# Seven half-size products for eight in the first channel product of the last batch

## The chip, the cores and the metric

The kernel runs on one core of one Trainium2 chip. A core has five engines with instruction queues of their own, each working in the order in which its instructions were written: TensorE (PE, matrix products, which land in PSUM), Vector (DVE), Scalar (ACT), GpSimd (POOL) and SyncE (SP, which here only starts DMAs). PSUM has 16 KB for each of the 128 partitions, in eight banks of 512 fp32 columns. Products are read out of PSUM by Vector or Scalar; POOL works on SBUF alone in this kernel. The metric is the device time of one launch, in microseconds.

## The reference

Four batches, eight heads, 768 positions, head size 64. First comes attention in which each position sees a window of 128 positions and four sink positions; then a ResMLP block on the joined heads (`d_model` 512, hidden size 2048):

```python
x = attention(q, k, v)                      # (4, 768, 512)
a1 = alpha1 * x + beta1
u = x + lam * einsum('ts,bsd->btd', w_tok, a1)
a2 = alpha2 * u + beta2
out = u + lam * (maximum(a2 @ w_ch1, 0) @ w_ch2)
```

The change concerns `a2 @ w_ch1` of batch 3: 768 tokens by 512 channels times 512 by 2048.

## The kernel before

The kernel is a list of small tasks. Each task names the engines that may do it with a planner's cost for each, the tasks that it needs, and the buffers that it uses. Three tables fix everything in advance: `ORDER` (the order in which tasks are written into the engines' queues), `ENGINES` (which engine does each: a digit for ACT, DVE, PE, POOL, SP) and `HOMES` (which physical copy each buffer takes). `Plan.emit` (L54) walks `ORDER` and allocates each buffer from its pool when its first task is written. So no queue is sorted at run time, and an instruction that waits holds up all that were written behind it for its engine.

PSUM is one pool of six homes: four single banks `d` and two double banks `S`. Attention scores use `S`; all other products share `d`.

Batches overlap: while the channel products of batch b run, the attention of batch b+1 is mixed in. For batch 3 there is no next attention, so from its token products on only the ResMLP block remains. The stages of a batch that matter here:

- **Token product** (`tok`, L849): six tiles of six matmuls of 512 columns; Vector adds each to x (L868), Scalar or POOL casts the result to fp16 (L871), SP transposes it by DMA into `uT` (L920), and four affine steps for each half of 384 tokens apply alpha2 and beta2 (`uTx`, L914; the instructions are at L885 for Scalar and L887 for Vector).
- **First channel product** (`mlp1`, L933): for each half of 384 tokens and each of 16 slices of 128 hidden channels, four matmuls of 384 columns (L941) add up over the 512 channels in one `d` bank; one relu reads the bank and writes fp16 into `hT` (Scalar at L947 or Vector at L949). That is 32 groups of four matmuls and 32 relus.
- **Second channel product** (`prod`, L1022; matmuls at L1058): for batches 1 to 3 this is already done as seven half-size products P1 to P7 for eight (Strassen's scheme as Winograd orders it). Its sums over `hT` are made by Vector (`h_sums`, L983), its sums over `w_ch2` once, in batch 0 (`w2_sums`, L960; the instructions are at L973). Vector adds each product's bank to x (L1071, L1089 and others), and the rows are stored by DMA (L1077).

```python
for c in range(NC):
    nc.tensor.matmul(
        ph.t, w1f[:, c, fi * P : (fi + 1) * P],
        bu.t[:, c, chk * NTOK : (chk + 1) * NTOK], start=(c == 0), stop=(c == NC - 1))
```

In the written order, the last products of batch 2 (three each of P6, P5 and P3) stand between and behind the token tiles of batch 3, and the first groups of batch 3's channel product are mixed with the last of them.

Of the kernel before, what the change touches and what calls it, by code (L numbers as in the profile page):

```python
# [7 lines left out]
FP32 = mybir.dt.float32  # L8
# [25 lines left out]
class Plan:  # L34
# [19 lines left out]
    def emit(self, order, engines, homes, idles):  # L54
# [7 lines left out]
        for i in order:  # L62
# [6 lines left out]
            for b in t.uses:  # L69
                if b.t is None:  # L70
                    pool, shape, dtype = self.pools[b.kind]
                    b.t = pool.tile(b.shape or shape, b.dtype or dtype,
                                    tag=f"{b.kind}_{b.home}", bufs=1, name=b.name)
# [4 lines left out]
def kernel(  # L78
# [17 lines left out]
    nc = tc.nc  # L96
# [21 lines left out]
    ctx.enter_context(tc.manual_schedule())  # L118

# [19 lines left out]
        "S": (ps, [P, 2, 512], FP32),  # L139
# [3 lines left out]
        "rec": 2, "u16": 4, "uT": 1, "hT": 2, "wst": 4, "d": 4, "S": 2, "pt": 3, "tm": 1,  # L143
# [54 lines left out]
    for r in range(NR):  # L198
# [97 lines left out]
        "1111333333302002002132132002132002102020101212010321213120301212131201012121312010121213"  # L296
# [550 lines left out]
    pch = {}  # L847

    def tok(p, b, ti):  # L849
        pt = Buf("S" if (b, ti) == (0, 5) else "d", None, None, f"tok{b}_{ti}")  # L850
        bx = x[b, ti]

        def bank():
# [483 lines left out]
```

## Time and profile before

| | before |
|---|---|
| median of three runs | 253.14 us (252.94 to 253.52) |
| the profiled execution: its time | 252.88 us |
| its span, first to last instruction | 251.0 us |
| TensorE busy | 245.5 us, 2167 matmuls |
| Vector, Scalar, POOL busy | 192.7, 131.4, 107.0 us |
| matmuls of L941, all four batches | 512 |

The times are those of whole launches; the span is what the trace of one of them shows, and the 1.88 us between the two lie before the first and after the last instruction. In rows of instruction groups, "x77 | 36.7, 492 | 34.3" means 77 instructions, 36.7 us busy, 492 ns for one on average, and 34.3 us in which the engine stood idle just before one of them; an arrow names what ended most of that. In rows of the timeline the first two numbers are the start and the length in us, and a bracket at the end gives the idle time just before. Instructions of one kind that follow each other are merged there, with their count at the end; they overlap a little, so a row of three is shorter than three times the length of one. In rows of one source line, "414/424/1108" are the shortest, the median and the longest in ns.

### The profile page before, as it was taken

Reading aid. Unit: us, or ns where it says so; the run is one execution under the profiler, and the core shown is the slowest. Engines: PE = TensorE matmul, PEld = TensorE weight load, DVE = VectorE, ACT = ScalarE, POOL = GpSimd, SP = SyncE. Lnnn points to the kernel's source line nnn. Section 1 sums busy time; section 2 is a strip of 40 time slices with the busy share of each in tenths; the row PEclk is TensorE's granted clock in tenths of the full one; section 3 lists DMA queues with packets and bytes.
Section 4 is the critical chain, followed back from the end, with each engine's and each line's share of the span. In section 5 each row is a group of like instructions: output and inputs, shape, how many; then the busy total and the mean of one; then the engine's idle time right before and its main releaser. Section 6 shows DMA issues by size and latency. Waiting matters only on the chain.

```text
span 251.0 us, 5521 instructions
## 1 busy us (share of the span) xinstructions
PE 245.5 (98%) x2167; PEld 160.7 (64%) x2167; DVE 192.7 (77%) x402; ACT 131.4 (52%) x218; POOL 107.0 (43%) x125
## 2 busy tenths in 40 slices
PE   8899999999999999999999999999999999999994
PEld 8654655675555544566787686567667676657884
DVE  6798987778788886688789986677689985218884
ACT  2399935788986025687751445556660235543000
POOL 8818724967866516432872040065563130000010
PEclk9999999999999999999999999999999999999999
DMA  6999999999999996896479364420000136200025
GB/s 210 211 260 352 225 177 298 362 355 284 218 207 229 222 200 154 168 258 153 108 159 187 63 129 147 135 63 2 3 0 3 21 69 190 100 0 3 22 65 167
DMA packets 86561, 38.79 MB, mean 155 GB/s; under 512 B 73588, under 2 KB 81276, under 8 KB 86536
## 3 DMA queue, kind: packets, MB, share of 16 engines
q1 hardware_dynamic: 67696, 29.37, 49.4%
q10 hardware_dynamic: 15096, 5.80, 9.8%
q0 software_dynamic: 3744, 3.28, 8.2%
q8 instruction: 17, 0.28, 0.5%
q14 instruction: 8, 0.07, 0.1%
HBM read 29.91 MB, written 6.29 MB: 144 GB/s over the span
## 4 chain that ended last, share of the span: by engine, by line
PE 90%; ACT 4%; DVE 3%; issue 2%; DVEq 0%; ACTq 0%
PE h L941 32%; PE P L1058 22%; PE tok L861 12%; PE ch L1128 8%; PE pv L727 4%; PE S L626 4%; PE idle L148 2%; PE tp L516 1%; ACT wt L823 1%; ACT E L648 1%; DVE qkT L157 1%; PE S L621 1%; PE tp L513 1%; PE pv L720 1%; PE sk L558 1%
## 5 line engine op out<-in xcount | busy, mean ns | idle before, releaser
L941 PE MATMUL h<-uT,w1f 128*128 128x384 f16 x512 | 89.3, 326 | 0.1
L941 PEld LDWEIGHTS <-w1f 128*128 128x128 f16 x512 | 48.4, 98 | 31.9 <-issue 2.0
L947 ACT ACTIVATE hT<-h 128x384 f16<-128x384 f32 x77 | 36.7, 492 | 34.3 <-PE h L941 30.6
L949 DVE TENSOR_SCALAR hT<-h 128x384 f16<-128x384 f32 x51 | 27.4, 552 | 23.8 <-PE h L941 23.3
L1058 PEld LDWEIGHTS <-hT 128*128 128x128 f16 x408 | 39.3, 98 | 7.0 <-DVE hT L1001 0.7
L648 ACT ACTIVATE E<-S 128x1024 f16<-128x1024 f32 (+1 forms) x39 | 37.8, 1002 | 6.3 <-PE S L626 5.3
L771 POOL TENSOR_TENSOR tm<-x,la_b 128x512 f32<-128x512 f32 x18 | 24.7, 1372 | 22.2 <-DVE xh L774 12.0
L861 PE MATMUL tok<-xh,wtokT 128*128 128x512 f16 x144 | 33.2, 379 | 0.0
L1058 PE MATMUL P<-w2f,hT 128*128 128x256 f16 x216 | 26.7, 273 | 0.0
L155 ACT CAST u<-x 128x512 f16<-128x512 f32 x17 | 10.3, 616 | 28.0 <-DVE x L868 26.9
L1071 DVE TENSOR_TENSOR x<-x,P 128x256 f32<-128x256 f32 x45 | 18.1, 417 | 7.2 <-PE P L1058 6.6
L1094 POOL TENSOR_TENSOR x<-x,pt 128x256 f32<-128x256 f32 x4 | 4.0, 993 | 46.0 <-DVE pt L1089 46.0
L1058 PE MATMUL P<-w2s,hT 128*128 128x256 f16 x192 | 23.3, 273 | 0.0
L861 PEld LDWEIGHTS <-wtokT 128*128 128x128 f16 x144 | 13.8, 98 | 14.8 <-issue 0.2
L1128 PE MATMUL ch<-w2f,hT 128*128 128x512 f16 x96 | 22.7, 379 | 0.0
L753 DVE TENSOR_TENSOR x<-pv,rec 128x256 f32<-128x256 f32 x48 | 20.4, 425 | 1.7
L155 ACT CAST n<-nat 128x768 f16<-128x768 f32 x20 | 16.2, 830 | 8.5 <-DVE vs L580 6.6
L868 DVE TENSOR_TENSOR x<-x,tok 128x512 f32<-128x512 f32 x24 | 16.0, 682 | 3.7 <-PE tok L861 3.5
L727 PEld LDWEIGHTS <-E 128*128 128x128 f16 x328 | 15.2, 97 | 4.9 <-issue 1.1
L727 PE MATMUL pv<-vfs,E 128*128 128x65 f16 x328 | 17.7, 194 | 0.0
L588 POOL TENSOR_SCALAR_AFFINE_SELECT E<-E 128x512 f16<-128x512 f16 x12 | 8.8, 753 | 17.7 <-ACT E L648 17.7
L157 POOL CAST vfs<-vnat 128x512 f16<-128x512 f32 x18 | 13.4, 750 | 4.2 <-PE pv L727 4.2
(133 smaller groups left out, 338.9 us busy)
## 6 DMA issues: line engine op xcount, KB each, us to landing
wst_w<-in_moe_w_ch_dram SPq DMA_DIRECT2D x8, 512.0 KB, 7.2
nat<-in_q_dram SPq DMA_DIRECT2D x10, 384.0 KB, 4.2
nat<-in_k_dram SPq DMA_DIRECT2D x10, 384.0 KB, 8.0
vnat<-in_v_dram SPq DMA_DIRECT2D x14, 256.0 KB, 6.2
out_dram<-x SPq DMA_DIRECT2D x11, 256.0 KB, 3.1
wtn<-in_moe_w_tok_dram SPq DMA_DIRECT2D x6, 384.0 KB, 4.8
w1f<-in_moe_w_ch_dram POOLq DMA_DIRECT2D x4, 512.0 KB, 10.6
out_dram<-x ACTq DMA_DIRECT2D x7, 256.0 KB, 4.7
```

The source lines that it names most:

```text
L155: nc.scalar.copy(o, i)
L648: nc.scalar.activation(eT.t, pS.t[:, :, 0 : n * w].rearrange("p e (i w) -> p e i w", i=n), AF.Exp, scale=scale)
L727: nc.tensor.matmul(po.t[:, hl, :], eT.t[:, e_, off + i, c : c + P], vf[j][:, h, :], start=(r < 2 and n == 0), stop=(n == len(parts) - 1 an ...
L753: nc.vector.tensor_mul(bx.t[:, 4 * G : 4 * G + 4, :], po.t[:, :, 0:D], rec.t.to_broadcast([P, 4, D]))
L771: engine[e].tensor_mul(bt.t, bx.t.rearrange("p h d -> p (h d)"), la1_b)
L861: nc.tensor.matmul(bank(), wtokT[:, si, ti * P : (ti + 1) * P], hs[si].t, start=(si == 0), stop=(si == NR - 1))
L941: nc.tensor.matmul(ph.t, w1f[:, c, fi * P : (fi + 1) * P], bu.t[:, c, chk * NTOK : (chk + 1) * NTOK], start=(c == 0), stop=(c == NC - 1))
L947: nc.scalar.activation(bh.t[:, fi, :], ph.t, AF.Relu)
L949: nc.vector.tensor_scalar_max(bh.t[:, fi, :], ph.t, 0.0)
L1058: nc.tensor.matmul(pc.t, hh[:, nt * P : (nt + 1) * P], w(fi), start=(first and n_ == 0), stop=(n_ == HF - 1), skip_group_check=True)
L1071: nc.vector.tensor_add(row(bx)[:, cols], row(bx)[:, cols], pc.t)
L1128: nc.tensor.matmul(pc.t, bh.t[:, fi, nt * P : (nt + 1) * P], w2f[:, fi, :], start=(fi == 0), stop=(fi == NF - 1))
```

## The change

The weights and the input of batch 3's first channel product are each cut into four blocks: the 512 channels in two halves, the 2048 hidden channels in two halves, the 768 tokens in two halves. Eight block products are replaced by seven.

- **Sums of the weights** (`w1_sums`): S1 to S4, four sums or differences of blocks, each made in four pieces of 512 fp16 elements per partition: 16 instructions, all on Vector. They go into the four `wst` buffers, in which batch 3's q and k were staged. In the written order they stand in batch 2: three behind the last products of batch 1 (ahead of the relu that leaves Vector idle at 154 us in the trace before), two ahead of the next relus, seven about where Vector is idle at 161 us, and the last four behind the exponential of the fifth key block, ahead of the normalising at 179 us.
- **Sums of the input** (`u_sums`): T1 to T4, 768 fp16 elements per partition each, T1 and T2 on Vector, T3 and T4 on POOL, once all affine steps that they read are done.
- **Products** (`mlp1_pair`): slices i and i+8 of the hidden channels form a pair, eight pairs in all. A pair has seven groups of two matmuls of 384 columns. Four of them (P1, P6, P7, P4) go one after the other into one bank A, and the bank is read in between: copied into a second bank B (k1), copied to SBUF (k2), added to another product (a22), and passed through the relu (r21). P2 adds onto the copy in B (relu r11). P5 goes into a third bank, is copied to SBUF (k5), and P3 adds onto it (a12). The results of the two adds get their relu as a clip in SBUF. So a pair has seven reads of PSUM of 384 columns and two clips, where it had four relus. By the engine table the 56 reads are 31 on Scalar and 25 on Vector, and the 16 clips eight each on POOL and Vector, one Vector clip of them behind the last product of the pairs.
- **PSUM**: the double banks `S` get a pool of their own, opened first. When the first buffer of the new kind `A` is written, that pool is closed and a pool of four single banks opens in its place, with waits tile by tile. Two token tiles of batch 3, the fourth and the fifth, use `A` banks as well.
- **Order**: the six token tiles of batch 3 stand together, with nothing in between; nine products of batch 2 follow, with the first P1 groups of four pairs among the last of them. Two P1 products of the second channel product stand between the last groups of the pairs.
- **Other tasks**: three relus of batch 2 move from Vector to Scalar, two of them near 158 us and one at 177 us of the trace before; one piece of `w2_sums` (T1 of the last group, near 90 us) moves from Vector to POOL; three products of batch 2 take other `d` banks.

The tables `ORDER`, `ENGINES` and `HOMES` are left out of the diff here.

```diff
@@ -69,6 +69,9 @@
             for b in t.uses:
                 if b.t is None:
                     pool, shape, dtype = self.pools[b.kind]
+                    if callable(pool):
+                        pool = pool()
+                        self.pools[b.kind] = pool, shape, dtype
                     b.t = pool.tile(b.shape or shape, b.dtype or dtype,
                                     tag=f"{b.kind}_{b.home}", bufs=1, name=b.name)
             t.fn(e)
...
+    scope = tc.tile_pool(name="psS", bufs=1, space=bass.MemoryType.PSUM, reuse_waits="tile")
+    psS = scope.__enter__()
+
+    def single():
+
+        scope.__exit__(None, None, None)
+        return ctx.enter_context(
+            tc.tile_pool(name="psA", bufs=1, space=bass.MemoryType.PSUM, reuse_waits="tile"))
...
         "d": (ps, [P, 512], FP32),
-        "S": (ps, [P, 2, 512], FP32),
+        "S": (psS, [P, 2, 512], FP32),
+        "A": (single, [P, 512], FP32),
...
-        "rec": 2, "u16": 4, "uT": 1, "hT": 2, "wst": 4, "d": 4, "S": 2, "pt": 3, "tm": 1,
+        "rec": 2, "u16": 4, "uT": 1, "hT": 2, "wst": 4, "d": 4, "S": 2, "A": 4, "pt": 3, "tm": 1,
...
-        pt = Buf("S" if (b, ti) == (0, 5) else "d", None, None, f"tok{b}_{ti}")
+        pt = Buf({(0, 5): "S", (3, 3): "A", (3, 4): "A"}.get((b, ti), "d"), None, None, f"tok{b}_{ti}")
...
+    HPAIR = (3,)
+    aS = {}
+    uD = {}
+    def w1_sums(p):
+        a11, a12 = w1f[:, 0:2, 0 : DFF // 2], w1f[:, 2:4, 0 : DFF // 2]
+        a21, a22 = w1f[:, 0:2, DFF // 2 : DFF], w1f[:, 2:4, DFF // 2 : DFF]
+        for s in ("S1", "S2", "S3", "S4"):
+            aS[s] = Buf("wst", [P, 2, DFF // 2], FP16, f"w1{s}")
+        for s, sub_, i0, i1, need in (("S1", 0, a21, a22, None), ("S2", 1, "S1", a11, "S1"),
+                                      ("S3", 1, a11, a21, None), ("S4", 1, a12, "S2", "S2")):
+            for g in range(4):
+                f = slice(256 * g, 256 * g + 256)
+                def f_(e, s=s, sub_=sub_, i0=i0, i1=i1, f=f):
+                    r0, r1 = [aS[z].t if isinstance(z, str) else z for z in (i0, i1)]
+                    op = engine[e].tensor_sub if sub_ else engine[e].tensor_add
+                    op(aS[s].t[:, :, f], r0[:, :, f], r1[:, :, f])
+                done["a" + s, g] = add(
+                    p, {POOL: 2500, DVE: 700}, f_,
+                    [done["w1", i] for i in range(4)] + ([done["a" + need, g]] if need else []),
+                    [aS[s]] + ([aS[need]] if need else []), port=True)
+    def u_sums(p, b):
+        bu = uT[b, 0]
+        b11, b12 = (lambda: bu.t[:, 0:2, 0:NTOK]), (lambda: bu.t[:, 0:2, NTOK:S])
+        b21, b22 = (lambda: bu.t[:, 2:4, 0:NTOK]), (lambda: bu.t[:, 2:4, NTOK:S])
+        for s in ("T1", "T2", "T3", "T4"):
+            uD[b, s] = Buf("n16", [P, 2, NTOK], FP16, f"uD{b}{s}")
+        c11, c12, c21, c22 = [[(chk, c), (chk, c + 1)] for c in (0, 2) for chk in range(2)]
+        for s, i0, i1, need, parts in (("T1", b12, b11, None, c11 + c12), ("T2", b22, "T1", "T1", c22),
+                                       ("T3", b22, b12, None, c12 + c22), ("T4", b21, "T2", "T2", c21)):
+            def f_(e, s=s, i0=i0, i1=i1):
+                r0, r1 = [uD[b, z].t if isinstance(z, str) else z() for z in (i0, i1)]
+                engine[e].tensor_sub(uD[b, s].t, r0, r1)
+            done["u" + s, b] = add(
+                p, {DVE: 500, POOL: 1900}, f_,
+                [done["uT", b, chk, c] for chk, c in parts]
+                + ([done["u" + need, b]] if need else []),
+                [uD[b, s], bu] + ([uD[b, need]] if need else []), port=True)
+    def mlp1_pair(p, b, i):
+        bu = uT[b, 0]
+        if i == 0:
+            for chk in range(2):
+                hT[b, chk] = Buf("hT", None, None, f"hT{b}_{chk}")
+        h0, h1 = hT[b, 0], hT[b, 1]
+        k_ = i + NF // 2
+        bA = Buf("A", [P, NTOK], FP32, f"hA{b}_{i}")
+        bB = Buf("d", [P, NTOK], FP32, f"hB{b}_{i}")
+        bE = Buf("d", [P, NTOK], FP32, f"hE{b}_{i}")
+        bU = Buf("E", [P, NTOK], FP32, f"hU{b}_{i}")
+        bV = Buf("E", [P, NTOK], FP32, f"hV{b}_{i}")
+        A = lambda: bA.t
+        w = lambda c, f: w1f[:, c, f * P : (f + 1) * P]
+        g = i // 2
+        def mm(name, o, ws, xs, start, stop, after, uses):
+            def f_(e, name=f"{name}.{i}"):
+                for n_ in range(2):
+                    nc.tensor.matmul(o(), ws(n_), xs(n_), start=start and n_ == 0, stop=n_ == 1,
+                                     skip_group_check=True)
+            return add(p, {PE: 326}, f_, after, uses)
+        def tok_(c, chk):
+            return bu.t[:, c, chk * NTOK : (chk + 1) * NTOK]
+        def sums(s, n_):
+            return aS[s].t[:, n_, i * P : (i + 1) * P]
+        def relu(name, o, pt, after, uses):
+            def f_(e, name=f"{name}.{i}"):
+                if e == ACT:
+                    nc.scalar.activation(o(), pt(), AF.Relu)
+                else:
+                    nc.vector.tensor_scalar_max(o(), pt(), 0.0)
+            return add(p, {ACT: 395, DVE: 480}, f_, after, uses)
+        def plus(name, o, i0, i1, after, uses):
+            def f_(e, name=f"{name}.{i}"):
+                nc.vector.tensor_add(o(), i0(), i1())
+            return add(p, {DVE: 480}, f_, after, uses)
+        def clip(name, o, after, uses):
+            def f_(e, name=f"{name}.{i}"):
+                engine[e].tensor_scalar_max(o(), o(), 0.0)
+            return add(p, {POOL: 600, DVE: 250}, f_, after, uses, port=True)
+        w1_ = [done["w1", z] for z in range(4)]
+        B_ = lambda: bB.t
+        E_ = lambda: bE.t
+        c11, c21 = (lambda: h0.t[:, i, :]), (lambda: h0.t[:, k_, :])
+        c12, c22 = (lambda: h1.t[:, i, :]), (lambda: h1.t[:, k_, :])
+        half = [done["uT", b, 0, c] for c in range(NC)]
+        m1 = mm("P1", A, lambda n_: w(n_, i), lambda n_: tok_(n_, 0), True, True, w1_ + half, [bA, bu])
+        k1 = add(p, {ACT: 395, DVE: 480}, lambda e, k=f"k1.{i}": copy(e, bB.t, A()), [m1], [bA, bB])
+        m2 = mm("P2", B_, lambda n_: w(2 + n_, i), lambda n_: tok_(2 + n_, 0), False, True, w1_ + half + [k1], [bB, bu])
+        done["h", b, 0, i] = relu("r11", c11, B_, [m2], [bB, h0])
+        m6 = mm("P6", A, lambda n_: sums("S2", n_), lambda n_: uD[b, "T2"].t[:, n_], False, True,
+                [k1, done["aS2", g], done["uT2", b]], [bA, aS["S2"], uD[b, "T2"]])
+        k2 = add(p, {ACT: 395, DVE: 480}, lambda e, k=f"k2.{i}": copy(e, bU.t, A()), [m6], [bA, bU])
+        m5 = mm("P5", E_, lambda n_: sums("S1", n_), lambda n_: uD[b, "T1"].t[:, n_], True, True,
+                [done["aS1", g], done["uT1", b]], [bE, aS["S1"], uD[b, "T1"]])
+        m7 = mm("P7", A, lambda n_: sums("S3", n_), lambda n_: uD[b, "T3"].t[:, n_], False, True,
+                [k2, done["aS3", g], done["uT3", b]], [bA, aS["S3"], uD[b, "T3"]])
+        k5 = add(p, {ACT: 395, DVE: 480}, lambda e, k=f"k5.{i}": copy(e, bV.t, bE.t), [m5], [bE, bV])
+        a22 = plus("a22", c22, A, lambda: bV.t, [m7, k5], [bV, bA, h1])
+        done["h", b, 1, k_] = clip("r22", c22, [a22], [h1])
+        m4 = mm("P4", A, lambda n_: w(2 + n_, k_), lambda n_: uD[b, "T4"].t[:, n_], False, True,
+                w1_ + [a22, done["uT4", b]], [bA, uD[b, "T4"]])
+        done["h", b, 0, k_] = relu("r21", c21, A, [m4], [bA, h0])
+        m3 = mm("P3", E_, lambda n_: sums("S4", n_), lambda n_: tok_(2 + n_, 1), False, True,
+                [k5, done["aS4", g]] + [done["uT", b, 1, c] for c in range(NC)], [bE, aS["S4"], bu])
+        a12 = plus("a12", c12, E_, lambda: bU.t, [m3, k2], [bE, bU, h1])
+        done["h", b, 1, i] = clip("r12", c12, [a12], [h1])
...
+        if b in HPAIR:
+            m1 = [("us",)] + [("hp", i) for i in range(NF // 2)]
         seq += m1
+        if b == HPAIR[0]:
+            w1_sums(w0 - 50)
         if b in STRASSEN:
             def two(u, w):
                 return [("pr", a, nt) for a, nt in ((u, 0), (u, 1), (w, 0), (u, 2), (w, 1), (w, 2))]
 
             seq += two("P1", "P2")
-            i = seq.index(("m1", 1, 8))
+            i = seq.index(("pr", "P1", 0) if b in HPAIR else ("m1", 1, 8))
             seq[i:i] = [("hs", "S3")]
             i = seq.index(("pr", "P1", 0))
             seq[i:i] = [("hs", "S1")]
...
                 p -= PAR["hs"] if args[0] == "S3" else PAR["s2"]
             if what == "pr" and args[0] in ("P7", "P4"):
                 p -= PAR["p7"]
-            {"tok": tok, "uT": uTp, "m1": mlp1, "m2": mlp2, "hs": h_sums, "pr": prod}[what](p, b, *args)
+            {"tok": tok, "uT": uTp, "m1": mlp1, "m2": mlp2, "hs": h_sums, "pr": prod,
+             "us": u_sums, "hp": mlp1_pair}[what](p, b, *args)
```

More of the change, by code (lines that the diff above doesn't have):

```diff
@@ L295 @@
         "1212020212120202120212020212121202020202022221022221422221022221422221022221013111111331"
-        "1111333333302002002132132002132002102020101212010321213120301212131201012121312010121213"
+        "1311333333302002002132132002132002102020101212010321213120301212131201012121312010121213"
         "1203212131212131213421342104011121042104213400012120202021202021212120202020212120202121"
@@ L299 @@
         "4400004440443333330404040404040404020201012120101212133201012121312030121213120101212133"
-        "2032121312121312104210421040001210421042104000121212120212121212121202120202021202121202"
-        "0202020112120202020212020112021212121211111212121212121213121112131214214214210214214044"
+        "2032121312121312104210421040001210421042104000121212120212020212121202120202021202121202"
+        "0202020112020202020212020112021212121211111212121212121213121112131214214214210214214044"
         "4404404404433333304040404043404040202010121203012121312010121213320103212131203012121312"
-        "0321213321213121042104210410002104213421341010202021202120212120212020202020212020212120"
-        "2020201120202120212020201120202142021421411112121212121212111421110213142102142142142102"
-        "10"
+        "0321213321213111111111111111112104210421040011210421342134010111332021202201120211202120"
+        "2211320211202121220132121320202022013202112021212201120213202020220112021320202122013202"
+        "11202020220132021111112020210202142141111212121212121211302133021314210214210214210214"
     )
@@ L312 @@
         "103100135301020081002011411421050103321a003101204000011011051003031104020013001303110312"
-        "0021102210121102223200511310123320031102032021035337572302312010320101420152002210101311"
-        "162103012154110041003020b005101119102307200030023123011223130032122313100100121232070302"
-        "1202002102135312330203"
+        "0021102210121102223200511310123320031102132301035337572302312010320101420152002210101311"
+        "162103012154110041003020b005101119102307200010323002312203102012310101300213420235320230"
+        "01141123522003311247002301135231000210"
     )
```

54 rows, old and new, of the table ORDER are left out of this document.

## The prediction

> **What bounds the kernel now.** I read the page first, then the chain of waits from 190 us on, then the busy time by stretches.
>
> ```profile
> span 251.0 us, 5521 instructions
> PE 245.5 (98%) x2167; PEld 160.7 (64%) x2167; DVE 192.7 (77%) x402; ACT 131.4 (52%) x218; POOL 107.0 (43%) x125
> ...
> PEclk9999999999999999999999999999999999999999
> ...
> PE 90%; ACT 4%; DVE 3%; issue 2%; DVEq 0%; ACTq 0%
> ```
> ```profile
> 192.91 3.88 PE tok L861 x18
> ...
> 210.01 18.85 PE h L941 x116
> ...
> 231.26 16.61 PE P L1058 x152
> ```
> ```profile
> 190.00:198.00 8.00, 8.00 (x58) 5.29 (x56) 8.00 (x13) 0.75 (x2) 0.67 (x1) 1.00 0.01 2
> 198.00:207.70 9.70, 9.70 (x73) 6.87 (x71) 8.21 (x16) 3.32 (x6) 3.07 (x4) 1.00 0.35 68
> 207.70:231.10 23.40, 23.40 (x155) 14.86 (x153) 9.71 (x19) 11.59 (x25) 0.00 (x0) 1.00 0.22 74
> ```
>
> TensorE is the bound: 98% busy, 90% of the chain, full clock in every slice. In the last batch (columns of the third fence: PE, PEld, DVE, ACT, POOL busy, then clock and DMA) it has no gap between 190 and 231 us. Vector has room in the first channel product (9.7 of 23.4 us) and none ahead of it (8.0 of 8.0). From the chain come the paces: a 384-column matmul 18.85/116 = 0.1625 us, a 512-column one 3.88/18 = 0.216 us (a token tile of six 1.29 us), a 256-column one 16.61/152 = 0.109 us (a product of eight 0.87 us).
>
> **What the change removes.** The first product of batch 3 is 32 groups of four matmuls, 128 in all; it becomes 8 pairs of seven groups of two, 112. That is 16 x 0.1625 = **2.60 us** of TensorE, on the path. Everything else is added work on other engines; it costs what it makes TensorE wait.
>
> **Evacuations in the pair stretch.**
>
> ```profile
> L947 ACT ACTIVATE hT<-h 128x384 f16<-128x384 f32 x77 | 36.7, 492 | 34.3 <-PE h L941 30.6
> L949 DVE TENSOR_SCALAR hT<-h 128x384 f16<-128x384 f32 x51 | 27.4, 552 | 23.8 <-PE h L941 23.3
> ```
> ```profile
> 157.84 1.48 DVE L949 TENSOR_SCALAR hT<-h 128x384 f16<-128x384 f32 x3
> ...
> 221.10 1.79 ACT L947 ACTIVATE hT<-h 128x384 f16<-128x384 f32 x4 [0.81 <-PE h L941]
> ...
> 227.43 0.96 DVE L999 TENSOR_TENSOR hS<-hT,hT 128x1536 f16<-128x1536 f16 x1
> ```
> ```profile
> L1071 DVE TENSOR_TENSOR x<-x,P x45: 406/420/423, 127.5 to 247.9; 128x256 f32<-128x256 f32 x45
> L887 DVE TENSOR_SCALAR uT<-uT,ab x9: 368/371/375, 99.6 to 213.9; 128x384 f16<-128x384 f16 x9
> L157 POOL CAST u<-x x7: 609/611/938, 41.3 to 205.1; 128x512 f16<-128x512 f32 x7
> ```
>
> 32 evacuations of 384 columns become 56 (31 on Scalar, 25 on Vector by the engine table), plus 16 clips. Back to back, one costs Scalar (1.79 - 0.49)/3 = 0.43 us and Vector (1.48 - 0.55)/2 = 0.47 us. Copies that write PSUM, or fp32 to SBUF, and adds of an fp32 operand have no row at 384 columns; L1071 adds 256 columns in 0.42, below the relu's 0.55, so I give all the relu's pace and bound them by 0.55 without overlap. A clip (fp16, SBUF to SBUF) is nearest L887 on Vector, 0.37. On POOL it is bounded by 0.61 (a cast of 512) above and three quarters of it, 0.46, below; either is harmless, since POOL has eight in 18 us.
>
> TensorE's time here is 112 x 0.1625 = 18.2 us, and two P1 products of the second channel product are mixed in: 18.2 + 1.7 = 19.9 us. Scalar needs 31 x 0.43 = 13.3. Vector needs 25 x 0.47 = 11.8, seven clips 2.6, two channel sums (L999) 1.9, together 16.3. So 82%: it fits, with 3.6 us to spare, but Vector goes in order and is the tightest. A bank's own chain is four groups with a read after each: 4 x (0.33 for two matmuls + 0.2 until the read starts + 0.55) = 4.3 us, 0.2 as an estimate from product P at 231.97 + 0.87 and its add at 233.04 below; with four A banks a pair may finish every 1.1 us, where TensorE needs 2.3. So banks are no limit. I take 0.2 us for stalls here, of 0 to 2.6 (the upper end: every Vector evacuation 0.55, every Vector clip kept waiting a POOL clip of 0.61: 13.8 + 6.9 + 1.9 = 22.5 against 19.9).
>
> ```profile
> 231.97 1.04 PE L1058 MATMUL P<-w2f,hT 128*128 128x256 f16 x8
> ...
> 233.04 0.42 DVE L1071 TENSOR_TENSOR x<-x,P 128x256 f32<-128x256 f32 x1 [0.26 <-PE P L1058]
> ```
>
> That upper end rests on this pair, where a Vector sum ran 1.71 us instead of 0.96 beside a POOL multiply:
>
> ```profile
> 189.40 1.27 POOL L771 TENSOR_TENSOR tm<-x,la_b 128x512 f32<-128x512 f32 x1
> ...
> 189.78 1.71 DVE L1000 TENSOR_TENSOR hT<-hT 128x1536 f16<-128x1536 f16 x1
> ```
>
> The Trainium skill ("SBUF — State Buffer", Who interferes with whom) speaks against the clips too: it says that Vector's two-port modes, open to tensor_scalar, lock GpSimd out and the reverse, while an instruction with at most one SBUF input outside them is free. The nine L887 rows, 368 to 375 ns, show none held, so no row here decides it for clips; by the rule the seven could wait their 0.61 each, by the rows nothing, and the adds from PSUM (L1071, 423 ns at most) are free by both.
>
> **Getting there: token tiles and input sums.**
>
> ```profile
> 192.07 0.68 DVE L774 TENSOR_TENSOR xh<-tm,lb_b 128x512 f16<-128x512 f32 x1
> ```
> ```profile
> L868 DVE TENSOR_TENSOR x<-x,tok x24: 674/681/689, 33.5 to 204.9; 128x512 f32<-128x512 f32 x24
> L973 DVE TENSOR_TENSOR w2s<-w2f,w2s x7: 414/424/1108, 49.4 to 92.4; 128x512 f16<-128x512 f16 x7
> L973 POOL TENSOR_TENSOR w2f<-w2f x2: 1153/1154/1154, 97.4 to 101.9; 128x512 f16<-128x512 f16 x2
> ```
> ```profile
> L920 SPq DMA_TRANSPOSE uT<-u x6: 1192/1214/1267, 198.9 to 207.0; - x6
> L885 ACT ACTIVATE uT<-uT,ab x5: 692/696/706, 204.1 to 212.3; 128x384 f16<-128x384 f16 x5
> ...
> DMA to landing us min/median/max: 2.5/2.5/2.5
> ```
>
> All six token tiles now run in a row from 192.9 to 200.7, then nine products of batch 2 (7.9 us) to 208.6, then four P1 groups and a P2 to 210.2; only then does a group need a sum. On Vector the first u follows the addition at 192.07, three channel sums of batch 2 (0.96) and two adds (0.42): 192.75 + 3.7 + 0.68 = 197.1, cast by 197.7. The six transposes queue on SP at 1.21 each, so the sixth starts at 203.8 and lands at 206.3; two affines on Scalar end by 207.7, T1 and T2 on Vector (768 elements, 1.5 x 0.42 = 0.63 each) by 209.0. T3 and T4 on POOL (1.5 x 1.15 = 1.7 each) end by 209.4 and 211.1, before P7 and P4 of the first pair, each of which has a read and another group ahead of it. Cover 1.2 us, cost 0; were T2 later than that, the rest would show. The stores of batch 2 stand behind all six transposes on SP, as before.
>
> **The weight sums in batch 2.** Sixteen Vector sums of 512 fp16 elements, the shape of L973, 0.42 each: 6.7 us where TensorE is full.
>
> ```profile
> 154.16 1.02 DVE L949 TENSOR_SCALAR hT<-h 128x384 f16<-128x384 f32 x2 [1.22 <-PE h L941]
> 156.11 1.21 DVE L949 TENSOR_SCALAR hT<-h 128x384 f16<-128x384 f32 x2 [0.93 <-PE h L941]
> ...
> 161.64 0.56 DVE L949 TENSOR_SCALAR hT<-h 128x384 f16<-128x384 f32 x1 [1.73 <-PE h L941]
> ...
> 179.19 0.18 DVE L752 RECIPROCAL rec<-pv 128x4 f32<-128x4 f32 x1 [1.15 <-PE pv L727]
> ```
> ```profile
> 163.78 1.22 POOL L588 TENSOR_SCALAR_AFFINE_SELECT E<-E 128x512 f16<-128x512 f16 x2 [13.21 <-ACT E L648]
> ...
> 184.24 1.40 POOL L588 TENSOR_SCALAR_AFFINE_SELECT E_None<-E_None 128x1024 f16<-128x1024 f16 x1 [1.57 <-ACT E_None L648]
> ```
>
> The order puts three, two and seven of them at idle places of 1.22, 0.93 and 1.73 us, and two relus near the third go to Scalar (2 x 0.47): 12 x 0.42 = 5.0 against 4.8. POOL is idle there until 163.78, so nothing holds them. The last four (1.7) stand before the normalising at 179.19, with 1.15 idle and one relu moved: 1.6. Behind them wait the reciprocal, and behind it the bank of the next group. Excess 0.2 + 0.1; I take 0.4 of 0 to 1.0 for order.
>
> **The moved w2 sum** goes from Vector (0.42) to POOL (1.15), right behind this POOL multiply:
>
> ```profile
> 87.33 1.27 POOL L771 TENSOR_TENSOR tm<-x,la_b 128x512 f32<-128x512 f32 x1 [0.87 <-DVE xh L774]
> ```
> ```profile
> 88.80 0.68 DVE L774 TENSOR_TENSOR xh<-tm,lb_b 128x512 f16<-128x512 f32 x1
> 89.40 0.87 DVE L973 TENSOR_TENSOR w2s<-w2f,w2s 128x512 f16<-128x512 f16 x2
> ```
> ```profile
> 90.32 4.05 PE L861 MATMUL tok<-xh,wtokT 128*128 128x512 f16 x18
> ```
>
> If POOL goes first, the addition at 88.80, which the token product at 90.32 needs, ends 1.15 later than 89.48: 0.3 late; if it goes second, 0. I take 0.2.
>
> **The pool.** The A banks are first written by the fourth token tile, 192.7 + 3 x 1.29 = 196.6. The last score was read before POOL masked it at 184.24. Twelve us of cover, cost 0; without it, a drain.
>
> **The sum.** -2.60 + 0.2 (pairs) + 0.4 (weight sums) + 0.2 (moved sum) = **-1.8 us**. The profiled execution took 252.88, its span 251.0 and 1.88 around it: 249.2 + 1.88 = 251.1. The median shown is 0.26 above that execution, so **251.3**.
>
> **Rivals.**
> 1. Vector becomes the bound of the pairs: late adds hold A banks, P4 and P7 wait. For it: in-order queue, locks. Against: 16.3 of 19.9. At half of the 2.6 bound, in place of the 0.2: 252.4; at the bound 253.7.
> 2. The weight sums slow batch 2 by more than the product saves. L973's largest is 1108 ns, and the change's own table prices a weight sum at 700 where the same shape in w2 has 345. At one element a cycle (start to start 88.80 to 89.40, 0.60), 16 x 0.60 = 9.6 against 6.4 of gaps: 3.2 lost, -2.6 + 0.4 + 3.2 = +1.0, **254.1**. It decides from 16s - 6.4 = 2.2, a sum of 0.54 us. Against: type, shape and operation are those of 0.42.
> 3. The pool doesn't follow tile by tile but drains the engines at 196.6: Vector was full from 190 to 198, so about a sum and an add, 1.3 us: 252.6.
> 4. Short groups leave gaps and the granted clock falls. Half the clock for one slice of 6.3 us costs 3.1: 254.4. Against: 9 in every slice, where products with as many bank changes run. The Trainium skill ("TensorE: Matmul & The Clock Gate", A second HAM failure mode: psum-queue depth-cycling) describes such a case, with gaps between groups; no run here shows it.
>
> **Chances.** Forecast 0.66, own range 250.5 to 252.3; rivals 0.16, 0.12, 0.04, 0.02. Measurement tells about 0.2%, 0.5 us. Faster: 0.65 of the forecast, half of the first and third rival, 0.75; slower: 0.12 + 0.02 and the end of the first, 0.15; 0.10 between. Range 250.4 to 253.4: the rival at 254.1, the clock and edges fall outside.
>
> **What would show it.** L941-like matmuls 16 fewer at 0.1625; no TensorE gap between 205 and 229; weight sums at 0.42 and the batch-2 products at most 0.5 later; T2 done before the second group that needs a sum; POOL's w2 sum near 89. It is wrong if gaps stand ahead of groups that wait for Vector adds, if weight sums last over 0.54, or if the first batches move.

## The result, and the profile after

The changed kernel takes 250.74 us (median of five, 250.49 to 250.94) against 253.14 (252.94 to 253.52): a ratio of 0.990, 95% interval 0.989 to 0.992. It is faster, by 2.40 us in the medians; the span of the profiled execution fell by 2.6 us, from 251.0 to 248.4 (that execution: 250.51). The forecast was 251.3.

The first lines of the page of the changed kernel, with busy time of each engine, and its share of the chain of waits by engine:

```profile
span 248.4 us, 5583 instructions
PE 242.9 (98%) x2151; PEld 159.2 (64%) x2151; DVE 208.0 (84%) x437; ACT 136.1 (55%) x229; POOL 126.0 (51%) x139
...
PEclk9999999999999999999999999999999999999999
...
PE 90%; ACT 4%; DVE 3%; issue 2%; DVEq 0%; ACTq 0%
```

TensorE has 16 matmuls fewer (2167 to 2151) and 2.6 us less to do, and still holds 90% of the chain at full clock in every slice. Vector does 15.3 us more, POOL 19.0, Scalar 4.7; the chain's shares are the ones of before, and in the last batch, shown next, none of the added work is on it.

From the chain of waits of the changed kernel, in order of time (start, length, engine and line):

```profile
192.98 7.77 PE tok L880 x36
200.75 4.37 PE P L1199 x40
...
226.23 0.87 PE P L1199 x8
227.10 0.65 PE hA L1041 x4
227.75 17.48 PE P L1199 x160
245.23 0.02 issue
245.25 0.42 DVE x L1212
```

The token tiles of the last batch start at 192.98, 0.07 us later than before: all sixteen weight sums and the moved w2 sum lie ahead of this point, and left no mark beyond that. From there to TensorE's last matmul it is 245.23 - 192.98 = 52.25 us, before 247.87 - 192.91 = 54.96. So 2.71 us are gained in this stretch, 2.60 of them the 16 matmuls; the other 0.11 us lie in the nine products of batch 2, which by the pieces of the two chains took 8.04 us while they stood between the token tiles and take 7.93 now.

Busy time by stretches in the changed kernel (PE, PEld, DVE, ACT, POOL, then clock and DMA):

```profile
198.00:205.00 7.00, 7.00 (x54) 5.12 (x53) 6.78 (x12) 2.47 (x4) 2.12 (x4) 1.00 0.48 94
205.00:209.80 4.80, 4.80 (x42) 3.87 (x40) 4.80 (x12) 1.87 (x4) 2.54 (x2) 1.00 0.58 190
209.80:227.60 17.80, 17.80 (x115) 10.96 (x113) 16.58 (x36) 12.61 (x30) 12.01 (x10) 1.00 0.13 46
```

TensorE has no gap in any of them. In the pairs (the last row) Vector is busy for 16.58 of 17.80 us, 93%; POOL, idle there before, has 12.01.

### The profile page after: what moved, and what is told of

It is laid out like the page before. It is cut to its first block, busy times and chain, and to the rows that moved or that the text cites. A ratio compares the mean times of both kernels' runs of the same rounds, so it can differ in the third digit from the quotient of the medians.

```text
span 248.4 us, 5583 instructions
## 1 busy us (share of the span) xinstructions
PE 242.9 (98%) x2151; PEld 159.2 (64%) x2151; DVE 208.0 (84%) x437; ACT 136.1 (55%) x229; POOL 126.0 (51%) x139
## 4 chain that ended last, share of the span: by engine, by line
PE 90%; ACT 4%; DVE 3%; issue 2%; DVEq 0%; ACTq 0%
PE h L960 24%; PE P L1199 22%; PE tok L880 12%; PE ch L1269 8%; PE hA L1041 4%; PE pv L746 4%; PE S L645 4%; PE idle L161 2%; PE hE L1041 2%; PE tp L535 1%; ACT wt L842 1%; ACT E L667 1%; PE hB L1041 1%; DVE qkT L170 1%; PE tp L532 1%
## 5 line engine op out<-in xcount | busy, mean ns | idle before, releaser
L960 PE MATMUL h<-uT,w1f 128*128 128x384 f16 x384 | 68.0, 326 | 0.1
L960 PEld LDWEIGHTS <-w1f 128*128 128x128 f16 x384 | 35.9, 98 | 24.0 <-issue 2.0
L966 ACT ACTIVATE hT<-h 128x384 f16<-128x384 f32 x58 | 27.9, 492 | 21.5 <-PE h L960 17.9
L968 DVE TENSOR_SCALAR hT<-h 128x384 f16<-128x384 f32 x38 | 20.4, 553 | 8.1 <-PE h L960 7.7
L170 POOL CAST u<-x 128x512 f16<-128x512 f32 x7 | 4.6, 663 | 26.1 <-DVE x L887 16.9
L170 POOL CAST vfs<-vnat 128x512 f16<-128x512 f32 x18 | 13.9, 778 | 5.1 <-PE pv L746 4.2
```

What stands on the lines that cost most here:

```text
L170: engine[e].tensor_copy(o, i)
L960: nc.tensor.matmul(ph.t, w1f[:, c, fi * P : (fi + 1) * P], bu.t[:, c, chk * NTOK : (chk + 1) * NTOK], start=(c == 0), stop=(c == NC - 1))
L966: nc.scalar.activation(bh.t[:, fi, :], ph.t, AF.Relu)
L968: nc.vector.tensor_scalar_max(bh.t[:, fi, :], ph.t, 0.0)
```

## The experiments

The theory: the change is worth the 16 matmuls that it takes from TensorE, and all that it adds lies beside TensorE's work. The rivals: the additions do cost something that a gain elsewhere covers; or they were close to costing more (Vector in the pairs, the weight sums, the first input sums). For small effects I also compare a **stretch**, from the start of batch 2's first channel product to the start of Vector's last addition. It leaves out the loads of the first batches. Before it is 152.01 to 247.89, 95.88 us; in the changed kernel 152.10 to 245.25, 93.15. In the runs below the kernel before had a median of 253.47 us (first four) and 253.53 (last four). TensorE's waits are read in two ways. A bracket in a timeline gives its idle time; but a matmul's record reaches some 0.16 us past the start of the next one (eight of 384 columns last 1.46 us in the timeline, 1.30 by the pace), so a wait puts all later matmuls back by the idle time and up to 0.17 us more. I give this **shift** where it is needed: how much later than in the changed kernel a group starts, both counted from the start of the stretch.

**1. Sixteen matmuls put back.** The two matmuls of P1 in each pair are issued twice, the second time over the first; what is computed stays the same.

```diff
-                for n_ in range(2):
+                for n_ in (0, 1, 0, 1) if name.startswith("P1") else (0, 1):
```

> The changed kernel with each pair's P1 group issued twice into the same bank (the second time overwrites the first), so the 16 saved matmuls are back and everything else stays. Theory A (the time follows TensorE's issue time, all added work is covered): 16 x 0.1625 = +2.6 us on the changed kernel's 250.74, so 253.3, no different from the kernel before. Theory B (the pairs are already paced by their evacuations, TensorE only looks full): a part of the added matmuls fills waits, +1 us or less, 251.0 to 251.8.

Measured: 253.39 us, 1.000 of the kernel before (0.998 to 1.002). The stretch is 152.39 to 248.08, 95.69 us, 2.54 more than in the changed kernel. With TensorE's work put back the gain is gone, but for 0.19 us of the stretch: it is the matmuls, and all the rest of the change together is worth nothing that can be measured.

**2. All clips on Vector.** The engine table gives the eight clips of POOL to Vector.

```diff
-        "2211320211202121220132121320202022013202112021212201120213202020220112021320202122013202"
-        "11202020220132021111112020210202142141111212121212121211302133021314210214210214210214"
+        "2211120211202121220112121120202022011202112021212201120211202020220112021120202122011202"
+        "11202020220112021111112020210202142141111212121212121211302133021314210214210214210214"
```

> The changed kernel with the eight clips of POOL on Vector instead. A Vector clip took 0.25 us in the changed kernel, so Vector's 16.6 us between 209.8 and 227.6 become up to 18.6 of 17.8. Theory A (a sum over a stretch does not decide, only a matmul that waits does; the channel sums of 0.95 us each can slip behind the stretch): 250.7 to 251.2. Theory B (Vector is the bound of the pairs as soon as its sum passes the stretch): 250.74 + 0.8 or more, 251.5 to 252.5.

Measured: 250.96 us, 0.991 (0.987 to 0.994); the stretch is 93.17 us, 0.02 more. The pairs' stretch of this kernel, and its clips by line:

```profile
209.80:227.60 17.80, 17.80 (x115) 11.08 (x114) 17.33 (x43) 12.25 (x28) 3.31 (x2) 1.00 0.16 59
```
```profile
L1066 DVE TENSOR_SCALAR hT<-hT x16: 249/251/260, 213.8 to 230.0; 128x384 f16<-128x384 f16 x16
```

Eight clips more on Vector bring it to 17.33 of 17.80 us, 97%, and TensorE still has no gap: at this load Vector is not the bound yet. Having clips on POOL is not needed for the time.

**3. One copy of each pair from Scalar to Vector.** The copy k1 (the read of P1 that P2 waits for) goes from Scalar to Vector in all eight pairs.

```diff
-        "0321213321213111111111111111112104210421040011210421342134010111332021202201120211202120"
-        "2211320211202121220132121320202022013202112021212201120213202020220112021320202122013202"
-        "11202020220132021111112020210202142141111212121212121211302133021314210214210214210214"
+        "0321213321213111111111111111112104210421040011210421342134010111332121202201120211212120"
+        "2211320211212121220132121321202022013202112121212201120213212020220112021321202122013202"
+        "11212020220132021111112020210202142141111212121212121211302133021314210214210214210214"
```

> The changed kernel with the eight k1 copies (first bank to second bank) on Vector instead of Scalar: 8 x 0.47 = 3.8 us more on Vector, 20.4 in a stretch of 17.8. Theory A: some 2 us of channel sums and clips can slip behind the stretch, the rest shows as TensorE waiting for k1 before P2 and P6: +0.6 to 2.2, 251.3 to 252.9. Theory B: Vector's whole excess shows, 2.6 or more, 253.3 and up.

Measured: 252.53 us, 0.997 (0.996 to 0.999); the stretch is 152.43 to 247.13, 94.70 us, 1.55 more than in the changed kernel. Two stretches of time and, from the timeline, one group of matmuls with its wait:

```profile
205.00:209.80 4.80, 4.43 (x39) 3.53 (x37) 4.80 (x12) 1.31 (x2) 1.91 (x2) 1.00 0.42 131
209.80:229.50 19.70, 19.12 (x121) 11.60 (x120) 19.42 (x45) 9.86 (x23) 12.29 (x10) 1.00 0.15 56
```
```profile
214.91 0.48 PE L1041 MATMUL hA<-uD3T,w1S 128*128 128x384 f16 x2 [0.56 <-DVE hB L170]
```

Eight copies at 0.47 are 3.8 us more on Vector, and it is now busy 19.42 of 19.70 us. TensorE is idle for 0.37 us ahead of the pairs, where a product of batch 2 waits for a late Vector addition, and for 0.58 in them, 0.56 of it for a copy (hB). The shift grows by 0.47 us at the first of these waits, by 0.72 at the second and by 0.36 in small steps behind it: together the 1.55 of the stretch. Of 3.8 us, 1.55 showed, so some 2.2 still found cover: Vector's room in the changed kernel is between the 1.2 us that it is idle in the pairs and these 2.2.

**4. Each weight sum made twice.** The sum is written a second time over itself; the result stays the same.

```diff
-                    op(aS[s].t[:, :, f], r0[:, :, f], r1[:, :, f])
+                    for _ in range(2):
+                        op(aS[s].t[:, :, f], r0[:, :, f], r1[:, :, f])
```

> The changed kernel with each of the 16 weight sums in batch 2 made twice: 16 x 0.34 = 5.4 us more on Vector. By the count of idle places (6.4 us, of which 5.4 are taken already): 4.4 us lost, 255.1. If the banks and the work written ahead give TensorE more slack than the idle places show, less: +1 to 3, 251.7 to 253.7. If Vector's place in batch 2 does not matter at all: 250.7.

Measured: 260.32 us, 1.028 (1.025 to 1.032); the stretch is 102.69 us, 9.54 more than in the changed kernel and far more than expected. Two things were missed. First, the price of a repeated sum: from the timelines of Vector, the changed kernel, then this one:

```profile
160.23 1.43 DVE L993 TENSOR_TENSOR w1S<-w1f 128x512 f16<-128x512 f16 x4
```
```profile
153.58 2.47 DVE L994 TENSOR_TENSOR w1S<-w1f 128x512 f16<-128x512 f16 x6
163.47 4.01 DVE L994 TENSOR_TENSOR w1S<-w1f 128x512 f16<-128x512 f16 x8
183.86 4.00 DVE L994 TENSOR_TENSOR w1S<-w1f,w1S 128x512 f16<-128x512 f16 x8
```

In the changed kernel each sum after the first costs (1.43 - 0.42)/3 = 0.34 us. A repeat starts only after the sum whose place it writes again has ended, so a sum and its repeat take 0.34 + 0.45 us from start to start; that gives the 2.47 us for six. The rows of eight are longer for another reason: in each of them two sums last 0.85 and 0.74 us instead of 0.42, while POOL is at work on a mask, which in the changed kernel comes when the sums are done. The sums of this kernel by line, and that work of POOL:

```profile
L994 DVE TENSOR_TENSOR w1S<-w1f x16: 416/424/852, 153.6 to 166.7; 128x512 f16<-128x512 f16 x16
L994 DVE TENSOR_TENSOR w1S<-w1f,w1S x8: 411/424/853, 183.9 to 187.4; 128x512 f16<-128x512 f16 x8
```
```profile
165.66 1.55 POOL L607 TENSOR_SCALAR_AFFINE_SELECT E<-E 128x512 f16<-128x512 f16 x2 [14.37 <-ACT E L667]
185.24 1.55 POOL L607 TENSOR_SCALAR_AFFINE_SELECT E<-E 128x512 f16<-128x512 f16 x2 [1.85 <-ACT E L667]
```

In all Vector does 9.0 us more (208.0 to 217.0), not 5.4; its time in weight sums rises from 5.7 to 14.0. Second, the clock. TensorE in the changed kernel, and the same two groups here:

```profile
163.83 1.46 PE L960 MATMUL h<-uT,w1f 128*128 128x384 f16 x8
...
166.00 0.61 PE L645 MATMUL S<-qkT 64*128 64x256 f16 x8
```
```profile
168.33 2.79 PE L960 MATMUL h<-uT,w1f 128*128 128x384 f16 x8 [2.56 <-DVE x L1213]
...
172.08 0.61 PE L645 MATMUL S<-qkT 64*128 64x256 f16 x8
```

And the stretches around that wait and around a second one (the column after POOL is the granted clock):

```profile
164.70:168.11 3.41, 1.07 (x5) 0.39 (x4) 3.32 (x7) 0.88 (x1) 2.45 (x4) 1.00 0.00 0
168.11:171.52 3.41, 3.19 (x14) 1.43 (x14) 2.42 (x6) 0.62 (x1) 0.40 (x1) 0.50 0.00 0
171.53:174.94 3.41, 3.41 (x43) 2.42 (x42) 2.33 (x8) 1.69 (x4) 1.84 (x2) 1.00 0.43 117
185.18:188.59 3.41, 1.15 (x18) 0.76 (x15) 3.20 (x8) 1.82 (x3) 1.55 (x2) 1.00 0.00 0
188.60:192.01 3.41, 3.41 (x12) 1.60 (x11) 1.97 (x5) 0.00 (x0) 1.26 (x1) 0.50 0.00 0
```

TensorE stood for 2.56 us, and then the granted clock was 0.50 for 3.41 us: eight matmuls took 2.79 us instead of 1.46. Against the changed kernel the first group is 168.33 - 163.83 = 4.50 us late and the second 172.08 - 166.00 = 6.08, so the low clock cost 1.58 us beside the wait. A second wait of 2.26 us did the same (0.50 for 3.41 us, 1.68 us lost). The waits themselves come to 6.3 us (shifts of 0.60, 0.56, 2.72 and 2.42), the clock to 3.3: 9.6, the 9.5 measured. The mean granted clock of this execution, 0.987, says the same: 1.3% of 258.6 us is 3.4. It is not always as much: of the four executions two had 0.987 and 0.986 (260.66 and 261.07 us), and two 0.993 (259.79 and 259.99), half the loss of clock.

**5. Only one set of weight sums made twice.** Since run 4 mixed the two, the four sums S3 alone are repeated.

```diff
-                    op(aS[s].t[:, :, f], r0[:, :, f], r1[:, :, f])
+                    for _ in range(2 if s == "S3" else 1):
+                        op(aS[s].t[:, :, f], r0[:, :, f], r1[:, :, f])
```

> The changed kernel with only the four pieces of S3 made twice: 4 x 0.4 = 1.6 us more on Vector at the third idle place of batch 2 (160 to 162 us). Without a slack beyond the idle places (2.7 us there with the two moved relus, of which seven sums take 2.4): 1.3 us lost, 252.0. If free banks and what is written ahead carry TensorE on for half a microsecond or more, as in the doubled run, where 1.4 us more on Vector cost TensorE 0.5: 0.4 to 0.9 lost, 251.1 to 251.6.

Measured: 252.21 us, 0.996 (0.994 to 0.997); the stretch is 152.84 to 247.20, 94.36 us, 1.21 more, for 1.8 us more work on Vector. TensorE on the timeline of this kernel, and the stretch around:

```profile
165.07 0.81 PE L960 MATMUL h<-uT,w1f 128*128 128x384 f16 x4 [0.35 <-DVE x L1213]
...
166.40 0.82 PE L960 MATMUL h<-uT,w1f 128*128 128x384 f16 x4 [0.51 <-DVE x L772]
```
```profile
164.00:167.00 3.00, 2.14 (x12) 0.90 (x11) 2.90 (x7) 0.53 (x1) 2.39 (x4) 1.00 0.00 0
```

Groups of matmuls wait for ordinary additions that now come late behind the sums, and the clock stays at 1.00 through gaps of this size. The shift is 0.51 us at the first of these waits and 1.18 after the second. Against the idle places of the prediction (6.4 us) the account by the time of all weight sums on Vector is: 5.7 us, no loss; 7.4, a loss of 1.2; 14.0, 6.3 of waiting. So the loss starts about where the places are full. Closer than that the three kernels don't tell, since a sum fits or not at its own place: at the third (2.7 us, of which seven sums take 2.4) the 1.8 us more would lose 1.5, and 1.2 were lost.

**6. Two token tiles back in the shared banks.** Token tiles 3 and 4 of the last batch take d banks, as in the kernel before, instead of A banks.

```diff
-        pt = Buf({(0, 5): "S", (3, 3): "A", (3, 4): "A"}.get((b, ti), "d"), None, None, f"tok{b}_{ti}")
+        pt = Buf({(0, 5): "S"}.get((b, ti), "d"), None, None, f"tok{b}_{ti}")
```

> The changed kernel with the fourth and fifth token tile of batch 3 in d banks (2 and 3) instead of A banks of the pool that follows the scores'. In the changed kernel the second token tile, which holds bank 2, was read by Vector until about 197.2, and the fourth would start at 196.7. If those two A banks carry a part of the gain: TensorE waits 0.5 us there, 251.2 (251.0 to 251.5). If the banks of the token tiles do not matter: 250.7.

Measured: 251.66 us, 0.992 (0.990 to 0.995); the stretch is 93.83 us, 0.68 more. The token tiles on TensorE's timeline, of the changed kernel and then of this one:

```profile
192.82 7.93 PE L880 MATMUL tok<-xh,wtokT 128*128 128x512 f16 x36
```
```profile
197.70 4.05 PE L880 MATMUL tok<-xh,wtokT 128*128 128x512 f16 x18 [0.48 <-DVE x L887]
```

With A banks all six tiles follow each other; with d banks the fourth waits 0.48 us for Vector's addition that empties its bank, a shift of 0.65 and the only wait of TensorE in this stretch. So a part of the pool's worth is in the token tiles, not in the pairs. And nothing drained at the change of pools: the fourth tile, the first to write an A bank, has no gap ahead of it.

**7. The first two input sums on POOL.** T1 and T2 go from Vector to POOL.

```diff
-        "0321213321213111111111111111112104210421040011210421342134010111332021202201120211202120"
+        "0321213321213111111111111111112104210421040011210421342134010133332021202201120211202120"
```

> The changed kernel with the input sums T1 and T2 on POOL, in front of T3 and T4 there. POOL's T4 took 1.64 us, so T1 to T4 end at about 209.6, 211.2, 212.9 and 214.5 where they ended at 208.5, 209.3, 210.8 and 212.4. Theory A (only the cover of T2 counts, 0.8 us in the changed kernel): the first P6, which started at 210.14, waits until 211.3, and P7 a little more: +1.2 to 2.0, 251.9 to 252.7. If what is written ahead gives more slack than that: 250.7.

Measured: 252.73 us, 0.996 (0.994 to 0.998); the stretch is 94.70 us, 1.55 more. The first group that needs a sum, on TensorE's timeline, and POOL's rows of T1, T2 and T3:

```profile
212.04 0.48 PE L1041 MATMUL hA<-uD3T,w1S 128*128 128x384 f16 x2 [1.08 <-POOL uD3T L1013]
```
```profile
208.56 1.65 POOL L1013 TENSOR_TENSOR uD3T<-uT 128x768 f16<-128x768 f16 x1 [1.97 <-ACT uT L904]
210.29 1.70 POOL L1013 TENSOR_TENSOR uD3T<-uT,uD3T 128x768 f16<-128x768 f16 x1
211.95 1.64 POOL L1013 TENSOR_TENSOR uD3T<-uT 128x768 f16<-128x768 f16 x1
```

The group waits for T2, which ends at 211.99, and starts at 212.04, a shift of 1.25 us; T3, which ends at 213.59, adds 0.30 to it ahead of the group at 213.64. These two are the 1.55. In the changed kernel T2 ends on Vector at 209.34 and that group starts at 210.14, with no wait: 0.8 us of cover.

**8. The late block read first.** In batch 1's token tiles the matmul of the sixth block, the one that reads the addition that stands behind the moved w2 sum, goes first instead of last. The sums are the same, in another order.

```diff
-                for si in sis:
+                last = NR - 1
+                for si in [last] + list(range(last)) if b == 1 else sis:
```

> The changed kernel with the six matmuls of each token tile of batch 1 in another order: the one that reads the last addition to xh goes first instead of sixth. If the moved w2 sum was free because only the sixth matmul waits for that addition: the first token product of batch 1, at 90.34 in the changed kernel, now waits until the addition has ended at 90.46 and starts 0.15 to 0.3 later, and the time grows by that much at most. If the token product waited as a whole already, nothing moves.

A single execution: 250.63 us, span 248.6. Vector's addition and TensorE in the changed kernel (two engines), then here:

```profile
88.82 1.64 DVE L793 TENSOR_TENSOR xh<-tm,lb_b 128x512 f16<-128x512 f32 x1
...
90.34 4.05 PE L880 MATMUL tok<-xh,wtokT 128*128 128x512 f16 x18
```
```profile
88.91 1.64 DVE L793 TENSOR_TENSOR xh<-tm,lb_b 128x512 f16<-128x512 f32 x1
...
90.60 4.04 PE L881 MATMUL tok<-xh,wtokT 128*128 128x512 f16 x18
```

In the changed kernel the addition ends at 88.82 + 1.64 = 90.46 and the token product starts at 90.34, ahead of it: only the sixth matmul of a tile reads it, and that one's turn comes at 90.34 + 5 x 0.216 = 91.42, so nothing waits. With the order turned, the first matmul starts at 90.60, just after the addition's end at 90.55, and 0.17 us after the 20 matmuls ahead of it were issued (86.11 + 20 x 0.216 = 90.43). One time as a whole can't tell 0.17 us; the row does.

## Why the prediction was right

The time, the sign and the mechanism were right: a kernel bound by TensorE lost 16 matmuls and their 2.60 us (run 1: 2.54). The sum was -1.8, the span says -2.6, the medians -2.4; 250.74 lies near the lower end of the forecast's own range (250.5 to 252.3). All that was off is the three positive terms, 0.8 us together; each measured nothing.

- **Pairs, 0.2 us: 0.** Vector was busy for 93% of the stretch where the sum gave 82%, and the room was 1.2 us where it gave 3.6. Vector's work was summed well (16.58 us for 16.3), but TensorE's time beside it was not 19.9 us: four P1 groups (1.3 us) lie ahead of the 17.8, as the prediction says itself further on, and of the two P1 products of the second channel product only one (the row at 226.23, 0.87 us) stands between the groups. The pace of 0.47 for copies into PSUM held (start to start in run 3: 0.47). What failed is the notion that an in-order engine near its limit must stall TensorE a little; at 97% (run 2) it still did not.
- **The clips.** POOL's clip, bounded by 0.46 and 0.61, took 1.16 us, outside the bounds; Vector's took 0.25 where I had 0.37. The row of POOL's clips in the changed kernel (least, median and greatest duration in ns):

```profile
L1066 POOL TENSOR_SCALAR hT<-hT x8: 1162/1163/1807, 212.8 to 226.9; 128x384 f16<-128x384 f16 x8
```

  A cast of 512 columns from fp32 was the wrong neighbour for a clip on POOL. It cost nothing because eight clips are still only some 10 us of 18. The clips on Vector's timeline, and some of POOL's:

```profile
214.55 0.59 DVE L1066 TENSOR_SCALAR hT<-hT 128x384 f16<-128x384 f16 x3
219.36 0.51 DVE L1066 TENSOR_SCALAR hT<-hT 128x384 f16<-128x384 f16 x1
226.62 1.07 DVE L1066 TENSOR_SCALAR hT<-hT 128x384 f16<-128x384 f16 x3
228.54 0.25 DVE L1066 TENSOR_SCALAR hT<-hT 128x384 f16<-128x384 f16 x1
```
```profile
216.32 3.44 POOL L1066 TENSOR_SCALAR hT<-hT 128x384 f16<-128x384 f16 x3 [2.39 <-DVE hT L1061]
224.66 3.42 POOL L1066 TENSOR_SCALAR hT<-hT 128x384 f16<-128x384 f16 x3 [0.49 <-DVE hT L1061]
```

  Four of the eight Vector clips ran while POOL was at its clips, and three of these were held: they took 0.51, 0.44 and 0.55 us, the fourth 0.25 like the rest. With no clips on POOL none of sixteen was (run 2, 249 to 260). That agrees in direction with the Trainium skill ("SBUF — State Buffer", Who interferes with whom), by which each of them could have waited; the trace shows three that did.
- **Token tiles and input sums, 0: 0.** T2 ended at 209.34 for 209.0 predicted, the group that needs it came at 210.14 for 210.2: the cover was 0.8 where I had 1.2. The prediction's remark that a later T2 would show is borne out by run 7. T3 was off: 2.64 us on POOL, not 1.7.

```profile
L1013 POOL TENSOR_TENSOR uD3T<-uT x1: 2642/2642/2642, 208.2 to 208.2; 128x768 f16<-128x768 f16 x1
L1013 DVE TENSOR_TENSOR uD3T<-uT,uD3T x1: 546/546/546, 208.8 to 208.8; 128x768 f16<-128x768 f16 x1
L1013 POOL TENSOR_TENSOR uD3T<-uT,uD3T x1: 1644/1644/1644, 210.8 to 210.8; 128x768 f16<-128x768 f16 x1
```

  It ended at 210.84 for a group at 211.44, so it was still hidden, by 0.6 us where the prediction's 209.4 would have left 2. T3 ran while Vector made T1 and T2, and POOL's T4 after them took 1.64. In run 7, where no such sum ran on Vector beside it, T3 took 1.64 as well: the extra microsecond goes with the neighbours on Vector.
- **Weight sums, 0.4 us: 0.** The term's price was wrong: 0.42 is the duration of one, while back to back each after the first costs 0.34. So they kept Vector busy for 5.7 us, not 6.7, against 6.4 us of idle places, and fit. I used the start-to-start pace for relus and the duration for sums; it should have been the same for both. The places themselves were counted well, as far as run 5 tells.
- **Moved w2 sum, 0.2 us: 0.** The mechanism came as feared: POOL's sum went first and the addition ended 1 us later, 90.46. The step that failed is "which the token product at 90.32 needs": only its sixth matmul does (run 8). The prediction did not know this; that the late addition cost nothing was luck.
- **The pool, 0: 0.** Run 6 shows more: two A banks for token tiles save a wait that the prediction did not see, 0.68 us of the stretch.

The rivals: Vector as the bound did not come, and run 3 shows that it begins 1 to 2 us further on, and costs 1.55 us at 3.8 us more. The weight sums as the larger cost did not come; it is real once the sums overfill the places (runs 4 and 5). The draining pool did not come. The falling clock did not come through short groups: the clock is 1.00 in every stretch of the pairs. It came in run 4, by another way, after single waits of over 2 us.

## What to carry to other kernels

In a kernel bound by one engine, take its removed work at full price, and price the added work by whether it fits in the idle places, with the start-to-start time of a row of such instructions and not with one's duration; up to 97% of an in-order engine cost nothing here. Ask of a late operand which single instruction reads it: one that reads it sixth in a row may hide a delay of a microsecond. Past the fit the loss can be larger than the overflow, since long waits can also cost clock (run 4: 6.3 us of waiting, 9.5 lost).

## What was not expected of the hardware

After waits of 2.26 and 2.56 us TensorE's granted clock was 0.50 for 3.41 us, and some 1.6 us were lost each time; after waits of 0.35, 0.51 (run 5) and 1.08 us (run 7) it stayed at 1.00. The Trainium skill ("TensorE: Matmul & The Clock Gate", HAM oscillation — how this bites in real kernels) asks for no idle gap over about 3.4 us; here shorter gaps did it, and the measurement decides.

The length of one wait may not be what decides. In run 4's trace the clock changes at 168.11, 171.53, 188.59 and 192.01 us, each time a whole number of 3.41 us after the change before. In the 3.41 us just ahead of its two falls TensorE was busy for 1.07 and 1.15 us, 31 and 34%. Counted in the same steps from the trace's first clock record, the 3.41 us of run 7 with the longest wait (209.34 to 212.75) have 2.33 us, 68%, and TensorE's last ones in run 8 (243.89 to 247.30) 1.53, 45%; the clock was 1.00 in what the traces show behind both. This fits a clock that is set every 3.41 us by how busy TensorE was in the 3.41 before, with a limit between 34 and 45%; no run was made to test it.

A sum of 512 fp16 elements costs Vector 0.34 us in a row of independent ones, 0.45 behind one whose place it writes again, and up to 0.85 beside a mask on POOL (run 4). And POOL needs 1.16 us for a clip of 384 fp16 elements that Vector makes in 0.25.
